# Decoding 64-bit weights by two bit operations, and looking for values out of range later

## The chip, the cores and the metric

The kernel runs on one core of a Trainium2 chip. The metric is the device time in microseconds of one execution, taken as the median of several runs. The core has TensorE (PE; its loading of weights is PEld), VectorE (DVE), ScalarE (ACT), GpSimd (POOL), SyncE (SP), and 16 DMA engines. Each engine carries out its own instructions in the order in which they stand; engines wait for each other by semaphores. VectorE and ScalarE both read the matmul results in PSUM.

## The reference

Three stages follow one another, with 3072 tokens of 512 values (4 batches of 768, 8 heads of 64). The weights `w_in` (512x1024) and `w_out` (1024x512) and `g_ln` arrive as 64-bit floating-point numbers, read by the kernel as pairs of 32-bit words; all else matters here only in outline.

```python
def _attn_ref(q, k, v, n_sink, window):
    scores = scale * np.matmul(q, k.transpose(0, 1, 3, 2))
    keep = is_sink | in_window
    scores = np.where(keep, scores, -1000000000.0)
    ...
    return np.matmul(a, v).astype(np.float32)

def _moe_ref(x, w_in, w_out, g_ln):
    h = x @ w_in
    ...
    solu = h * sm
    ln = (solu - mu) / np.sqrt(var + 1e-06) * g_ln
    return (ln @ w_out).astype(np.float32)

def _moe2_ref(x, w_gate, w1, w2):
    logits = x @ w_gate
    expert_idx = np.argmax(logits, axis=1)
    ...
    for e in range(E):
        xe = x[mask]
        h = np.maximum(xe @ w1[e], 0.0)
        ye = h @ w2[e]
        out[mask] = gate_w[mask, None] * ye
```

## The kernel before, in words

**Three stages.** Attention goes in 32 units, each two heads by three blocks of 128 queries. A unit is loaded (`a_load`), split into a high and a low part (`a_split`), its scores are made and their exponentials taken (`a_scores`, L223, L224, L230), the probabilities are transposed (`a_trans`, `tp`, L277) and multiplied with the values (`a_out`, `av`, L299), and the result is split into `bxh` and `bxl` (L304, L305), which are the input of the next stage. Four units make the input of one block of three tiles of 128 tokens. The MLP goes in 24 tiles: `m_in` (L428 to L430) makes `h` by three matmuls for each of four `k`, where `k` needs the unit `k` of the block; `m_act` takes the softmax and the normalization; `m_out` (L498 to L500) multiplies with `w_out`, with the router's logits as eight columns more. The experts' stage takes the 8 experts one after the other, sorted by load: `f_in` makes `ht` and from it `hh` and `hl` (L833, L834), `x_trans` makes `xeh` and `xel` for the next expert (L791, L792), `f_out` makes `y`. Their weights (`wst`, 512 KB each, eight for an expert: four of w1, four of w2) come through SyncE's queue (L725) and are split by ScalarE (`wh`, L733) and VectorE or GpSimd (`wl`, L741).

**High and low.** Every product of 32-bit numbers is made of three products of shorter ones: high by high, high by low, low by high. That is why each operand is split into a part that ScalarE rounds and a part that VectorE gets by subtraction.

**Decoding of `w_in` and `w_out`.** 16 tiles (8 of each) of 128 rows by 512 values, 512 KB each, are loaded through ScalarE's queue (L322) into `w64`, a tile with three buffers (`WB`). `decode` makes 32-bit floats of them. VectorE takes away the upper bits of the high word and shifts it left by three (L326, into `dt` in PSUM), and joins the sign and the top bit of the exponent (L328, into `dec`). ScalarE turns the low word into its top three bits (L329, in place) and takes the size of the high word, read as a float (L331, into `dh`). GpSimd adds the three bits (L332), which rounds the number. VectorE at last multiplies by zero whatever is too small for a 32-bit float (L334). `load_w_in` splits the result into `wih` and `wil` (L342, L343), `load_w_out` scales it by `g_ln` and splits it into `woh` and `wol` (L372, L373), and makes the logits' columns by transposes and matmuls on TensorE (`wt`, L351 and L359) of the decoded tile. `dec` has four buffers.

**What sets the order.** The program is written out with the units of attention and the tiles of weights in turn (L1253 to L1263: one tile every six steps, the last eight from step 62 on), then the MLP's steps beside the attention's; a scheduler then puts each engine's instructions in the order in which they would be ready by its own model of time. So the order on an engine is fixed when the kernel is built, and each engine keeps to it, also where what it waits for comes late.

**A second path.** `flags` (L1007) makes two flags on the input's values; if one is set, the fallback functions (`general_attention` and the like, at the end) compute the result again in another way. With the inputs of this case they do not run.

## Time and profile before

| | before |
|---|---|
| median of 3 runs | 822.47 us (821.12 to 825.34) |
| profiled execution, device time | 825.15 us |
| its span, first to last instruction | 823.4 us |
| mean granted clock of TensorE | 0.985 |
| TensorE busy | 771.7 us (94%) |
| VectorE busy | 470.6 us (57%) |
| ScalarE busy | 471.9 us (57%) |
| GpSimd busy | 377.4 us (46%) |

The rows below come from the profile of that one execution. The windows view gives for each stretch the busy time of each engine, with the number of instructions in brackets, the granted clock of TensorE as a share of its full speed, the mean busy share of the 16 DMA engines, and the rate at which they moved data. Groups of instructions are named by line, engine and operation, with output and inputs by the program's names; behind a bar stand the busy time in us and the mean length of one in ns, and behind a second bar the time for which the engine sat idle just before them, and what ended it. The chain of waits follows the work that ended last back from its end, piece by piece. "x16" is the number of instructions.

### The profile page before, as it was taken

How to read it: one execution, taken by the hardware profiler on the slowest of the kernel's cores; microseconds unless marked ns; L12 is line 12 of the kernel's file. 1: busy time of each engine (PE TensorE's matmuls, PEld its weight loads, DVE VectorE, ACT ScalarE, POOL GpSimd, SP SyncE). 2: the span in 40 equal slices, each digit the busy share in tenths (PEclk: the TensorE clock that was granted, in tenths of full speed). 3: DMA queues.
4: the chain of work that ended last, by engine and by line, in shares of the span. 5: the costliest groups of instructions: out<-in, count | busy, mean ns of one | idle time of the engine just before them, and what ended most of it. 6: DMA issues, size and time to landing. Idle time of an engine off the chain costs nothing.

```text
span 823.4 us, 15551 instructions
## 1 busy us (share of the span) xinstructions
PE 771.7 (94%) x5002; PEld 669.7 (81%) x5002; DVE 470.6 (57%) x1742; ACT 471.9 (57%) x1256; POOL 377.4 (46%) x413
## 2 busy tenths in 40 slices
PE   3469999889999999999999998999999999999996
PEld 2148888778888887888888888989978889889885
DVE  6788674755857756658667458516324324334441
ACT  4786685665866866848757466225424333436442
POOL 4787356435454553554533202137335344434533
PEclk9995999999999999999999999999999999999998
DMA  7776366668545656664540073076264415642550
GB/s 243 227 220 183 101 158 108 164 115 137 136 111 151 132 160 128 131 140 128 126 112 28 27 178 119 14 246 207 59 221 150 137 49 161 204 177 80 191 171 28
DMA packets 77418, 114.37 MB, mean 139 GB/s; under 512 B 14154, under 2 KB 53516, under 8 KB 77328
## 3 DMA queue, kind: packets, MB, share of 16 engines
q1 hardware_dynamic: 69648, 91.02, 42.9%
q0 software_dynamic: 5088, 13.88, 4.9%
q10 hardware_dynamic: 2592, 8.39, 3.0%
q8 instruction: 42, 0.69, 0.4%
q14 instruction: 48, 0.39, 0.3%
HBM read 72.22 MB, written 13.28 MB: 104 GB/s over the span
## 4 chain that ended last, share of the span: by engine, by line
PE 78%; DMA 8%; DVE 6%; ACT 3%; issue 2%; POOL 1%; SPq 0%; POOLq 0%; ACTq 0%; DVEq 0%
PE ht L825 5%; PE ht L826 5%; PE ht L827 5%; PE x L498 5%; PE av L299 5%; PE h L428 5%; PE y L897 5%; PE x L500 5%; PE y L895 5%; PE y L896 5%; PE x L499 5%; PE h L429 5%; PE h L430 4%; PE s L223 3%; DMA w<-w_out 2%
## 5 line engine op out<-in xcount | busy, mean ns | idle before, releaser
L498 PE MATMUL x<-woh,lh 128*128 128x264 f32 (+1 forms) x384 | 111.4, 290 | 0.1
L230 ACT ACTIVATE P<-P,mx 128x144 f32<-128x144 f32 x192 | 78.7, 412 | 54.6 <-DVE mx L228 51.9
L500 PE MATMUL x<-woh,ll 128*128 128x264 f32 (+1 forms) x384 | 109.4, 286 | 0.0
L499 PE MATMUL x<-wol,lh 128*128 128x264 f32 (+1 forms) x384 | 109.0, 284 | 0.0
L733 ACT ACTIVATE wh<-wst 128x1024 fp32r<-128x1024 f32 x64 | 67.5, 1058 | 46.1 <-PE ht L826 26.3
L741 POOL TENSOR_TENSOR wl<-wst,wh 128x1024 fp32r<-128x1024 f32 x28 | 68.2, 2436 | 56.0 <-ACT wh L733 49.0
L741 DVE TENSOR_TENSOR wl<-wst,wh 128x1024 fp32r<-128x1024 f32 x36 | 54.7, 1524 | 46.5 <-ACT wh L733 46.4
L826 PE MATMUL ht<-xel,wh 128*128 128x288 f32 (+5 forms) x256 | 81.1, 318 | 0.0
L827 PE MATMUL ht<-xeh,wl 128*128 128x288 f32 (+5 forms) x256 | 81.0, 318 | 0.0
L188 POOL TENSOR_TENSOR lA<-qd,qA 128x384 fp32r<-128x384 f32 x29 | 29.7, 1024 | 110.1 <-ACT qA L186 102.8
L825 PE MATMUL ht<-xeh,wh 128*128 128x288 f32 (+5 forms) x256 | 79.9, 318 | 0.0
L428 PE MATMUL h<-wih,bxh 128*128 128x512 f32 x192 | 78.6, 410 | 0.8 <-DVE ll L481 0.8
L227 DVE COPY_PREDICATED s<-pick,s 128x128 f32<-128x128 int32 x160 | 45.5, 291 | 55.9 <-PE s L224 53.8
L895 PE MATMUL y<-wh,hh 128*128 128x512 f32 x192 | 77.0, 402 | 0.0
L429 PE MATMUL h<-wil,bxh 128*128 128x512 f32 x192 | 76.5, 398 | 0.0
L897 PE MATMUL y<-wh,hl 128*128 128x512 f32 x192 | 75.8, 396 | 0.0
L896 PE MATMUL y<-wl,hh 128*128 128x512 f32 x192 | 75.1, 392 | 0.0
L430 PE MATMUL h<-wih,bxl 128*128 128x512 f32 x192 | 74.3, 400 | 0.0
L498 PEld LDWEIGHTS x<-woh,lh 128*128 128x128 f32 x384 | 72.3, 188 | 1.6 <-DVE r L531 0.3
L499 PEld LDWEIGHTS x<-wol,lh 128*128 128x128 f32 x384 | 72.4, 189 | 0.8
L500 PEld LDWEIGHTS x<-woh,ll 128*128 128x128 f32 x384 | 72.3, 189 | 0.4 <-issue 0.2
L228 DVE CUSTOM_DVE_ANT_0 P<-s,mk 128x144 f32<-128x144 f32 x192 | 55.9, 301 | 12.9 <-PE s L224 6.8
(259 smaller groups left out, 2058.4 us busy)
## 6 DMA issues: line engine op xcount, KB each, us to landing
wst<-w SPq DMA_DIRECT2D x64, 512.0 KB, 5.4
x_d<-xrow SPq DMA_DIRECT2D x24, 264.0 KB, 2.5
qd<-qT SPq DMA_DIRECT2D x32, 192.0 KB, 3.5
qB<-qA SPq DMA_DIRECT2D x58, 96.0 KB, 4.1
lB<-lA SPq DMA_DIRECT2D x58, 96.0 KB, 2.4
kd<-kx SPq DMA_DIRECT2D x16, 280.0 KB, 3.2
w<-w_in ACTq DMA_DIRECT2D x8, 512.0 KB, 6.6
w<-w_out ACTq DMA_DIRECT2D x8, 512.0 KB
```

What stands on the lines that cost most here:

```text
L428: T.matmul(h, xh[k], wih[:, k, cs], start=(k == 0), stop=False)
L429: T.matmul(h, xh[k], wil[:, k, cs], start=False, stop=False)
L498: T.matmul(p[:, 0:n], lh[:, k, :], woh[:, k, c, 0:n], start=(k == 0), stop=False)
L499: T.matmul(p[:, 0:n], lh[:, k, :], wol[:, k, c, 0:n], start=False, stop=False)
L500: mm = T.matmul(p[:, 0:n], ll[:, k, :], woh[:, k, c, 0:n], start=False, stop=(k == 7))
L741: return (G if c % 2 and r else V).tensor_tensor(out=l_, in0=st_w.pop((r, which, c)), in1=raw(h_), op=ALU.subtract)
L825: T.matmul(o, wh[:, k, fs], xh(k), start=(k == 0), stop=False)
L826: T.matmul(o, wh[:, k, fs], xl(k), start=False, stop=False)
L827: T.matmul(o, wl[:, k, fs], xh(k), start=False, stop=(k == 3))
L895: T.matmul(o, hh[:, k, sl], wh, start=(k == 0), stop=False)
L896: T.matmul(o, hh[:, k, sl], wl, start=False, stop=False)
L897: T.matmul(o, hl[:, k, sl], wh, start=False, stop=(k == 7))
```

## The change

The weights' tiles are decoded by two operations on VectorE and one on ScalarE. ScalarE turns the low word into its top three bits by the factor `LOW3`. VectorE shifts the high word left by three and joins the three bits by an exclusive or (`dt`); the second operation takes the sign of the high word and joins it by an exclusive or, with 0x80000000 for a constant. The exponent is not brought to the range of a 32-bit float: the number comes out with its sign turned and a power of two too large, which the next operations take out, since they have a factor (`SC_IN`, `SC_OUT`, `SX`, `RAW`). L331, the sum on GpSimd and the clearing at L334 are gone. The subtractions that make `wil` and `bxl` become operations with a factor. `g_s` and `g_l` are `g_ln` by those factors. `w64` has four buffers (`WB`). The old way stays for the fallback (`flush=True`).

Without the clearing, values out of the range would be decoded wrongly. So in the experts' stage the 16 tiles are loaded again through SyncE's queue (`look_at_weights`, into a `w64` with two buffers), and VectorE takes the least and the greatest size of the high words, read as floats, of each tile (`chk`, 32 reductions). `flag_weights`, called before the last expert, reduces them (`far`), compares (`bad`), sums over the 128 rows by one matmul (`ct`), and raises both flags of the second path; the cast `flag_i` moves there from `flags`.

The diff, without the fallback's own part:

```diff
--- before.py
+++ after.py
@@ -28,7 +28,7 @@
 NPT, XBUFS, QKB, PKB, VB = 2, 8, 2, 2, 2
-WB, DB, EB, NXR, XGB = 3, 4, 2, 2, 6
+WB, DB, EB, NXR, XGB = 4, 4, 2, 2, 6
 PA = 3
@@ -44,7 +44,10 @@
 PART = [n % 128 if n % 128 in (32, 64) else 0 for n in ROOM]
-E_MIN = struct.unpack("<f", struct.pack("<I", 897 << 20))[0]
+E_MIN, E_ONE = [struct.unpack("<f", struct.pack("<I", e << 20))[0] for e in (897, 1023)]
+LOW3 = 7.4995 * 2.0 ** -32
+SC_IN, SC_OUT, SX = 2.0 ** 8, 2.0 ** 64, 2.0 ** -8
+RAW = -2.0 ** -128
@@ -301,13 +304,15 @@
         xl = xp.tile([128, 384], F32R, tag="xl", name="bxl", bufs=XBUFS)
-        A.activation(out=xh, in_=o[:, 0:384], func=AF.Copy)
-        V.tensor_tensor(out=xl, in0=o[:, 0:384], in1=raw(xh), op=ALU.subtract)
+        A.activation(out=xh, in_=o[:, 0:384], func=AF.Copy, scale=SX)
+        V.scalar_tensor_tensor(out=xl, in0=o[:, 0:384], scalar=SX, in1=raw(xh), op0=ALU.mult, op1=ALU.subtract)
         x_t.setdefault(n // 4, []).append((xh, xl))
...
     g_sb = const.tile([128, 8], F32, name="g_sb")
+    g_s = const.tile([128, 8], F32, name="g_s")
+    g_l = const.tile([128, 8], F32, name="g_l")
     wg_sb = const.tile([128, 4, NE], F32, name="wg_sb")
@@ -315,42 +320,55 @@
-    def decode(src, sb=None):
+    def decode(src, sb, flush):
...
         lo, hi = w[:, :, 0], w[:, :, 1]
-        t = dec_tile("dec")
         t0 = ps("dt").bitcast(I32)
-        V.tensor_scalar(out=t0, in0=hi, scalar1=0x07FFFFFF, scalar2=3, op0=ALU.bitwise_and,
-                        op1=ALU.logical_shift_left)
-        V.scalar_tensor_tensor(out=t, in0=hi, scalar=-0x40000000, in1=t0, op0=ALU.bitwise_and, op1=ALU.bitwise_or)
-        A.activation(out=lo, in_=lo.bitcast(U32), func=AF.Copy, scale=2.0 ** -29)
-        x = ps("dh")
-        A.activation(out=x, in_=hi.bitcast(F32), func=AF.Abs)
-        G.tensor_tensor(out=t, in0=t, in1=lo, op=ALU.add)
-        y = x if sb is None else sb
-        V.scalar_tensor_tensor(out=y, in0=x, scalar=E_MIN, in1=t.bitcast(F32), op0=ALU.is_ge, op1=ALU.mult)
+        y = ps("dh") if sb is None else sb
+        if flush:
...
+        else:
+            A.activation(out=lo, in_=lo.bitcast(U32), func=AF.Copy, scale=LOW3)
+            V.scalar_tensor_tensor(out=t0, in0=hi, scalar=3, in1=lo, op0=ALU.logical_shift_left, op1=ALU.bitwise_xor)
+            V.scalar_tensor_tensor(out=y.bitcast(I32), in0=hi, scalar=-0x80000000, in1=t0, op0=ALU.bitwise_and,
+                                   op1=ALU.bitwise_xor)
         return y
-    def load_w_in():
+    def load_w_in(flush=False):
+        sc = SC_IN * (1.0 if flush else RAW)
         for k in range(4):
             for c in range(2):
-                x = decode(a["w_in"].bitcast(I32)[128 * k:128 * k + 128, 1024 * c:1024 * c + 1024])
+                x = decode(a["w_in"].bitcast(I32)[128 * k:128 * k + 128, 1024 * c:1024 * c + 1024], None, flush)
                 h_ = wih[:, k, 512 * c:512 * c + 512]
-                A.activation(out=h_, in_=x, func=AF.Copy)
-                V.tensor_tensor(out=wil[:, k, 512 * c:512 * c + 512], in0=x, in1=raw(h_), op=ALU.subtract)
+                A.activation(out=h_, in_=x, func=AF.Copy, scale=sc)
+                V.scalar_tensor_tensor(out=wil[:, k, 512 * c:512 * c + 512], in0=x, scalar=sc, in1=raw(h_),
+                                       op0=ALU.mult, op1=ALU.subtract)
                 yield 0
-    def load_w_out():
+    def load_w_out(flush=False):
+        sc = SC_OUT * (1.0 if flush else RAW)
+        V.tensor_scalar(out=g_s, in0=g_sb, scalar1=sc, scalar2=None, op0=ALU.mult)
+        V.tensor_scalar(out=g_l, in0=g_sb, scalar1=1.0 / SC_OUT, scalar2=None, op0=ALU.mult)
+
         def logits(k, x):
...
             xt = dec_tile("xt").bitcast(F32).rearrange("p (a b) -> p a b", a=4)
-            A.activation(out=xt, in_=t.rearrange("p (a b) -> p a b", a=4), func=AF.Copy)
+            A.activation(out=xt, in_=t.rearrange("p (a b) -> p a b", a=4), func=AF.Copy, scale=sc)
             return k, xt
@@ -358,7 +376,7 @@
             wp = t[:, 0:NE]
-            gk = g_sb[:, k:k + 1]
+            gk = g_l[:, k:k + 1]
             V.tensor_scalar(out=woh[:, k, 0, 256:264], in0=wp, scalar1=gk, scalar2=None, op0=ALU.mult)
@@ -366,11 +384,11 @@
             x = dec_tile("dec").bitcast(F32)
-            decode(a["w_out"].bitcast(I32)[128 * k:128 * k + 128, :], x)
+            decode(a["w_out"].bitcast(I32)[128 * k:128 * k + 128, :], x, flush)
             h_ = woh[:, k, :, 0:256]
             p2 = x.rearrange("p (a b) -> p a b", a=2)
-            A.activation(out=h_, in_=p2, func=AF.Copy, scale=g_sb[:, k:k + 1])
-            V.scalar_tensor_tensor(out=wol[:, k, :, 0:256], in0=p2, scalar=g_sb[:, k:k + 1], in1=raw(h_),
+            A.activation(out=h_, in_=p2, func=AF.Copy, scale=g_s[:, k:k + 1])
+            V.scalar_tensor_tensor(out=wol[:, k, :, 0:256], in0=p2, scalar=g_s[:, k:k + 1], in1=raw(h_),
                                    op0=ALU.mult, op1=ALU.subtract)
@@ -500,7 +518,7 @@
                     yield 0.65
-            A.activation(out=xr[:, 256 * c:256 * c + 256], in_=p[:, 0:256], func=AF.Copy)
+            A.activation(out=xr[:, 256 * c:256 * c + 256], in_=p[:, 0:256], func=AF.Copy, scale=1.0 / SC_OUT)
             if c == 0:
@@ -831,8 +849,8 @@
                 A.activation(out=hh[:, f, gs], in_=o, func=AF.Relu)
-                V.scalar_tensor_tensor(out=hl[:, f, gs], in0=o, scalar=0.0, in1=raw(hh)[:, f, gs], op0=ALU.max,
-                                       op1=ALU.subtract)
+                hl_last[0] = V.scalar_tensor_tensor(out=hl[:, f, gs], in0=o, scalar=0.0, in1=raw(hh)[:, f, gs],
+                                                    op0=ALU.max, op1=ALU.subtract)
             yield
@@ -960,10 +978,13 @@
                 x_gather(r + 1)
+            (look_at_weights if more else flag_weights)()
             for _ in f_in(r):
...
                 pass
+            if more:
+                look_at_weights()
             if not more:
@@ -987,6 +1008,8 @@
                 w2 = w_load(r + 1, 2)
+            if r in (1, 2):
+                look_at_weights()
@@ -1014,8 +1037,45 @@
         V.tensor_tensor(out=flag[:, 1:2], in0=flag[:, 1:2], in1=flag[:, 0:1], op=ALU.max)
+        rest_blocks(False)
+
+    chk = const.tile([128, 2, 16], F32, name="chk")
+    look, seen, hl_last = [], [0], [None]
+
+    def look_at_weights():
+
+        while look:
+            i, w = look.pop()
+            with tc.issue_after(hl_last[0].ins):
+                for j, op in enumerate((ALU.min, ALU.max)):
+                    V.tensor_reduce(out=chk[:, j, i:i + 1], in_=w[:, :, 1].bitcast(F32), axis=AX.X, op=op,
+                                    apply_absolute_value=True)
+        i = seen[0]
+        if i < 16:
+            seen[0] += 1
+            k = i % 8
+            w = pool2["h"].tile([128, 512, 2], I32, tag="w64", name="w64", bufs=2)
+            with tc.issue_after(loaded[-1].ins):
+                SY.dma_start(out=w, in_=a["w_out"].bitcast(I32)[128 * k:128 * k + 128, :] if i < 8 else
+                             a["w_in"].bitcast(I32)[128 * (k // 2):128 * (k // 2) + 128,
+                                                    1024 * (k % 2):1024 * (k % 2) + 1024])
+            look.append((i, w))
+
+    def flag_weights():
+        look_at_weights()
+        assert seen[0] == 16 and not look
+        far = const.tile([128, 2], F32, name="far")
+        bad = const.tile([128, 1], BF16, name="bad")
+        V.tensor_reduce(out=far[:, 0:1], in_=chk[:, 0], axis=AX.X, op=ALU.min)
+        V.tensor_reduce(out=far[:, 1:2], in_=chk[:, 1], axis=AX.X, op=ALU.max)
+        V.tensor_scalar(out=far[:, 0:1], in0=far[:, 0:1], scalar1=E_MIN, scalar2=None, op0=ALU.is_lt)
+        V.scalar_tensor_tensor(out=bad, in0=far[:, 1:2], scalar=E_ONE, in1=far[:, 0:1], op0=ALU.is_ge, op1=ALU.max)
+        p = ps("ct")
+        T.matmul(p[:, 0:1], ones_b, bad, start=True, stop=True)
+        for j in range(2):
+            V.scalar_tensor_tensor(out=flag[:, j:j + 1], in0=p[:, 0:1], scalar=0.5, in1=flag[:, j:j + 1],
+                                   op0=ALU.is_ge, op1=ALU.max)
         V.tensor_copy(flag_i, flag)
-        rest_blocks(False)
```

Three places of the instruction order follow; names are those of the program with a running number, which differs between the two builds. In all of them an engine's rows are in the order of its execution.

ScalarE at the start of the program, before: loads of `w64` (a DMA that it issues), and the first uses of the tiles.

```order
L322 DMA w64_239<-w_in 128x1024
L322 DMA w64_301<-w_in 128x1024
L322 DMA w64_360<-w_in 128x1024
L329 ACTIVATE w64_239<-w64_239 128x512
L331 ACTIVATE dh_246<-w64_239 128x512
L329 ACTIVATE w64_301<-w64_301 128x512
L331 ACTIVATE dh_308<-w64_301 128x512
L322 DMA w64_435<-w_in 128x1024
L230 ACTIVATE P_208,sm_210<-P_208,mx_209 128x144 x3
L329 ACTIVATE w64_360<-w64_360 128x512
L331 ACTIVATE dh_367<-w64_360 128x512
```

The same place after:

```order
L327 DMA w64_242<-w_in 128x1024
L327 DMA w64_300<-w_in 128x1024
L327 DMA w64_355<-w_in 128x1024
L327 DMA w64_426<-w_in 128x1024
L343 ACTIVATE w64_242<-w64_242 128x512
L343 ACTIVATE w64_300<-w64_300 128x512
L233 ACTIVATE P_211,sm_213<-P_211,mx_212 128x144 x3
L355 ACTIVATE wih_68<-dh_245 128x512
L327 DMA w64_466<-w_in 128x1024
L343 ACTIVATE w64_355<-w64_355 128x512
L355 ACTIVATE wih_68<-dh_303 128x512
```

Four loads stand at the head in place of three, the row `dh<-w64` (L331) is gone behind each use, and the fifth and sixth load come with one tile's use between them.

TensorE where the first product `h` of the MLP stands, before: `wt` are transposes and logits of the w_out tiles (the tile `dec_1191` is the seventh of eight), `s` scores of attention.

```order
L359 MATMUL wt2_1294<-wg_sb_125,xt_1217 128x8 x4
L351 MATMUL wt_1301<-ident_78,dec_1191 128x128 x2
L223 MATMUL s_722<-kA_685,qA_681 128x272
L224 MATMUL s_722<-kA_685,lA_683 128x272
L223 MATMUL s_728<-kB_686,qB_682 128x272
L224 MATMUL s_728<-kB_686,lB_684 128x272
L351 MATMUL wt_1301<-ident_78,dec_1191 128x128 x2
L428 MATMUL h_1314<-wih_68,bxh_454 128x512
L429 MATMUL h_1314<-wil_69,bxh_454 128x512
L430 MATMUL h_1314<-wih_68,bxl_455 128x512
L428 MATMUL h_1314<-wih_68,bxh_576 128x512
L429 MATMUL h_1314<-wil_69,bxh_576 128x512
```

The same place after (`dec_1134` is again the seventh):

```order
L377 MATMUL wt2_1143<-wg_sb_127,xt_1095 128x8 x4
L369 MATMUL wt_1150<-ident_78,dec_1074 128x128 x4
L226 MATMUL s_589<-kA_531,qA_527 128x272
L227 MATMUL s_589<-kA_531,lA_529 128x272
L377 MATMUL wt2_1227<-wg_sb_127,xt_1155 128x8 x4
L369 MATMUL wt_1234<-ident_78,dec_1134 128x128 x4
L446 MATMUL h_1247<-wih_68,bxh_441 128x512
L447 MATMUL h_1247<-wil_69,bxh_441 128x512
L448 MATMUL h_1247<-wih_68,bxl_442 128x512
L446 MATMUL h_1247<-wih_68,bxh_555 128x512
L447 MATMUL h_1247<-wil_69,bxh_555 128x512
L226 MATMUL s_595<-kB_532,qB_528 128x272
```

The first `h` uses the first two units (`bxh_441`, `bxh_555`) here, where before it used three (`bxh_454`, `bxh_576`, `bxh_709`) in a row; the third unit's output `av` comes behind the eighth tile.

VectorE at the end of the first layer of the fifth expert, before:

```order
L834 SCALAR_TENSOR_TENSOR hl_9002<-ht_9102,hh_9001 128x384
L834 SCALAR_TENSOR_TENSOR hl_9002<-ht_9117,hh_9001 128x384
L834 SCALAR_TENSOR_TENSOR hl_9002<-ht_9132,hh_9001 128x384
L792 TENSOR_TENSOR xel_9148<-xt_9149,xeh_9147 128x4x128
L795 COPY gate_185<-xg_8995 128x1
L800 CAST ids_f_184<-idx_i_182 128x1
```

The same place after, with the four reductions between the last `hl` and the first `xel`:

```order
L852 SCALAR_TENSOR_TENSOR hl_8976<-ht_9076,hh_8975 128x384
L852 SCALAR_TENSOR_TENSOR hl_8976<-ht_9091,hh_8975 128x384
L852 SCALAR_TENSOR_TENSOR hl_8976<-ht_9106,hh_8975 128x384
L1051 TENSOR_REDUCE chk_200<-w64_8973 128x1 x2
L1051 TENSOR_REDUCE chk_200<-w64_9123 128x1 x2
L810 TENSOR_TENSOR xel_9126<-xt_9127,xeh_9125 128x4x128
L813 COPY gate_187<-xg_8965 128x1
L818 CAST ids_f_186<-idx_i_184 128x1
```

SyncE's queue at the same expert, before: the last load of its second layer's weights and the next expert's first-layer weights (`w1`).

```order
L725 DMA wst_9081<-w2 128x2x512
L725 ISA
L725 DMA wst_9189<-w1 128x4x256
L725 ISA
L725 DMA wst_9235<-w1 128x4x256
L725 ISA
L725 DMA wst_9281<-w1 128x4x256
L725 ISA
L725 DMA wst_9287<-w1 128x4x256
```

The same place after:

```order
L743 DMA wst_9055<-w2 128x2x512
L743 ISA
L743 DMA wst_9167<-w1 128x4x256
L1059 DMA w64_8973<-w_in 128x1024
L743 ISA
L743 DMA wst_9213<-w1 128x4x256
L1059 DMA w64_9123<-w_in 128x1024
L743 ISA
L743 DMA wst_9259<-w1 128x4x256
L743 ISA
L743 DMA wst_9265<-w1 128x4x256
```

Two loads of `w64` have come between the first and the third load of `w1`.

## Rows read from the trace of the kernel before

**Rows 1.** Windows of 20 us: PE, PEld, DVE, ACT, POOL busy, clock, DMA share, GB/s:

```profile
0.00:20.00 20.00, 7.22 (x20) 3.92 (x20) 13.34 (x54) 8.73 (x23) 9.43 (x54) 1.00 0.77 241
...
20.00:40.00 20.00, 8.78 (x25) 4.28 (x25) 14.78 (x47) 14.39 (x38) 15.01 (x17) 1.00 0.70 221
...
40.00:60.00 20.00, 12.38 (x72) 8.56 (x73) 17.06 (x47) 16.95 (x43) 15.51 (x14) 1.00 0.79 229
...
80.00:100.00 20.00, 19.82 (x117) 16.60 (x116) 13.52 (x58) 11.57 (x37) 8.59 (x12) 1.00 0.43 118
```

**Rows 2.** The waits, TensorE, 90 to 540 us: total, times, longest:

```profile
PE s L224 <- DMA lA<-lA: 2.5, 1, 2.5
```

**Rows 3.** The windows view, most of the experts' stage, columns as in 1:

```profile
540.00:800.00 260.00, 260.00 (x1571) 229.03 (x1570) 100.20 (x190) 111.69 (x200) 116.88 (x75) 1.00 0.49 160
```

**Rows 4.** The windows view, other stretches of the front, columns as in 1:

```profile
0.00:69.00 69.00, 35.99 (x156) 23.67 (x157) 53.32 (x173) 46.51 (x120) 45.86 (x91) 0.94 0.78 235
...
21.00:51.00 30.00, 14.01 (x55) 7.92 (x54) 24.33 (x68) 22.73 (x57) 22.95 (x24) 1.00 0.68 210
...
51.00:69.00 18.00, 13.90 (x81) 11.33 (x82) 14.76 (x50) 14.23 (x41) 13.48 (x14) 0.79 0.95 265
...
63.00:78.00 15.00, 13.83 (x66) 11.91 (x64) 14.12 (x36) 11.07 (x28) 11.74 (x11) 0.50 0.69 172
```

**Rows 5.** Chain of waits up to 110 us: start, length, what:

```profile
32.15 2.48 POOL dec L332 x2
...
41.85 1.30 POOL dec L332
...
59.37 4.75 DMA w<-w_out
```

**Rows 6.** The timeline, ScalarE: start, length, what, idle before it and releaser:

```profile
68.88 0.67 ACT L329 ACTIVATE w<-w 128x512 int32<-128x512 uint32 x1 [0.30 <-DMA w<-w_out]
```

**Rows 7.** The timeline, TensorE:

```profile
79.81 0.48 PE L428 MATMUL h<-wih,bxh 128*128 128x512 f32 x1
```

**Rows 8.** Instruction groups up to 90 us: busy, mean ns, idle before and releasers:

```profile
L332 POOL TENSOR_TENSOR dec<-dec,w 128x512 int32<-128x512 int32 x16 | 20.9, 1310 | 14.4 <-DVE dec L328 9.0 <-ACT xt L353 2.4 <-PE s L224 2.1
...
L326 DVE TENSOR_SCALAR dt<-w 128x512 int32<-128x512 int32 x16 | 11.0, 687 | 4.8 <-DMA w<-w_in 3.5 <-DMA w<-w_out 1.2
...
L328 DVE SCALAR_TENSOR_TENSOR dec<-w,dt 128x512 int32<-128x512 int32 x16 | 10.8, 678 | 0.0
...
L329 ACT ACTIVATE w<-w 128x512 int32<-128x512 uint32 x16 | 10.8, 677 | 18.2 <-DMA w<-w_in 11.8 <-DMA w<-w_out 6.4
...
L331 ACT ACTIVATE dh<-w 128x512 f32<-128x512 f32 x16 | 9.9, 622 | 0.0
...
L373 DVE SCALAR_TENSOR_TENSOR wol<-dec,g_sb,woh 128x512 fp32r<-128x512 f32 x8 | 8.4, 1056 | 4.5 <-ACT woh L372 4.5
...
L334 DVE SCALAR_TENSOR_TENSOR dh<-dh,dec 128x512 f32<-128x512 f32 x8 | 5.5, 691 | 0.0
...
L334 DVE SCALAR_TENSOR_TENSOR dec<-dh,dec 128x512 f32<-128x512 f32 x8 | 5.4, 676 | 0.0
```

**Rows 9.** Instruction groups, whole program, columns as in 8:

```profile
L434 DVE TENSOR_REDUCE sc<-h 128x1 f32<-128x512 f32 x48 | 32.3, 685 | 16.3 <-PE h L430 14.1 <-ACT e L462 2.1
...
L792 DVE TENSOR_TENSOR xel<-xt,xeh 128x512 fp32r<-128x512 f32 x25 | 17.2, 688 | 74.2 <-ACT xeh L791 74.1
```

**Rows 10.** The waits, ScalarE, 540 to 824 us:

```profile
ACT wh L733 <- DMA wst<-w: 3.5, 3, 1.6
```

**Rows 11.** The timeline, VectorE, end of the program:

```profile
793.41 1.15 DVE L801 TENSOR_TENSOR dst<-ids_f,pen 128x1 int32<-128x1 f32 x1
...
800.65 1.23 DVE L741 TENSOR_TENSOR wl<-wst,wh 128x1024 fp32r<-128x1024 f32 x1 [6.09 <-ACT wh L733]
```

**Rows 12.** The timeline, TensorE: two sets of six transposes:

```profile
54.11 0.88 PE L277 MATMUL tp<-ident,pk 128*128 128x128 f32 x6
...
73.33 1.49 PE L277 MATMUL tp<-ident,pk 128*128 128x128 f32 x6
```

16 lines of the change are left out of this document (13 added, 3 removed).

## The prediction

> **What bounds the kernel now.** I read the windows first, in stretches of 20 us. Over the first 60 us TensorE works 7.22, 8.78 and 12.38 us of each 20 [rows 1], so 31.6 us of it are idle; from 80 us on it is nearly full (19.82 of 20 [rows 1]). Over 90 to 540 us its largest wait on anything is 2.5 us in all [rows 2], and from 540 to 800 us it is busy 260.00 of 260.00 [rows 3]. So the end of the program can move in one way only: TensorE must get its work earlier in the first 80 us, or be made to wait later on. VectorE or GpSimd time saved anywhere else costs and earns nothing.
>
> Next I asked what holds the front. VectorE is busy 13.34, 14.78 and 17.06 of 20 there [rows 1], the highest of the helpers, and the 16 DMA engines are busy 0.78 of the first 69 us [rows 4]. The chain of waits goes through both: a piece of 4.75 us of waiting for a weight tile to land, and before it pieces of the GpSimd sum `dec` at L332 (2.48 us for two of them, 1.30 for another) [rows 5]. The reader should see the loop: a load needs a free one of three buffers, the buffer is given back by the last reader of the raw tile, which is the GpSimd sum at L332, and that sum waits for VectorE. The last of the 16 tiles is picked up by ScalarE at 68.88 us [rows 6], and the first matmul of the MLP starts at 79.81 us [rows 7]. It needs none of the w_out tiles, but it stands in TensorE's row behind the transposes and logits of seven of them.
>
> **The change part by part.**
>
> *Decoding, VectorE.* Per tile, L326, L328 and L334 (687, 678 and 691 or 676 ns, 16 of each [rows 8]) make 2.05 us. Two operations of 128x512 in their place, of the same kind as L328 (two inputs, 678 ns) make 1.36. That is 0.69 us by 16 tiles: 11.0 us less, all of it before 80 us. The low half of w_out, L373, takes 1056 ns on average against 678 for an operation of the same size and kind [rows 8]; the nearest reason in the trace is that GpSimd reads and writes beside it. GpSimd loses its 20.9 us of L332 [rows 8]; if half of the excess goes with it, 8 times 0.19, that is 1.5 us. VectorE: −12.5 us.
>
> *Decoding, ScalarE and GpSimd.* ScalarE loses 16 times L331, 9.9 us [rows 8], GpSimd 20.9. ScalarE had 18.2 us of waiting for tiles in front of L329 [rows 8], so of its saving I count nothing by itself. The GpSimd sum stood in the chain, and with it went the handovers between VectorE, ScalarE and GpSimd; the raw tile is now given back by the second VectorE operation.
>
> *The scale factors.* The power of two goes into operations that were there already (the scale of an activation, or a two-input subtraction that becomes one with a scalar, of the kind and size of L328). The 32 `bxl` operations change kind in the same way. The two 128x8 products `g_s` and `g_l` are done once. All together under 0.5 us on an engine that is not full; nothing in the sum.
>
> *The fourth buffer and the loads.* Bytes do not change in the front. The DMA engines are busy 0.68 of 21 to 51 us and 0.95 of 51 to 69 [rows 4]: in the first stretch they have 9.6 us free, because loads wait for buffers; in the second they are the limit. With four buffers, given back two handovers earlier, weights can use the free 9.6 us. All of the 69 us hold 53.8 us of transfers (0.78 by 69 [rows 4]), so even packed without a gap the last tile could not land much before 56 to 58 us, 11 to 13 us earlier. The order of ScalarE shows four loads at the head where there were three, and the next already behind the first use of one tile.
>
> Of the two limits the smaller decides: VectorE could give 12.5 us, the transfers 9.6. I take 9.6, as the stretch from 21 to 51 us is what the buffers govern. The lower end is 3.7 us, the two GpSimd pieces shown from the chain (2.48 and 1.30 [rows 5]) with every load where it was. The upper end is 16.5 us, 9.6 and the clock's 6.9 (below), half of TensorE's idle 31.6.
>
> There is a rule that speaks against the fourth buffer. The row shows the DMA engines at 0.95 where several loads are under way [rows 4]. The Trainium skill, page "DMA: Bandwidth & Descriptors", section "Issuing engines are not separate DMA queues", says that transfers of all issuing engines run on the same 16 engines and interleave. By that rule a fourth load at the head takes its time from the first three and from the first queries and keys: 512 KB at the 265 GB/s of 51 to 69 us are 2.0 us, and the sum would be 7.6 in place of 9.6. I don't take this, since those engines then have a gap later.
>
> *TensorE's order.* In both orders the first h matmul stands behind the logits of the seventh w_out tile; but ahead of it the changed order has two outputs of attention (`av`) in place of three, and behind it h products of five blocks with those two units before the fourth output comes. So TensorE gets h work sooner after the weights are there, and the third and fourth unit later. What it gains up to 90 us it keeps, as it is full behind. I put no further gain in the sum, and the later units into the last rival.
>
> *Looking for values out of range.* 16 loads of 512 KB more, and 32 reductions on VectorE, all in the experts' stage. The nearest row is the reduction of 512 values at L434, 685 ns [rows 9]: 32 times 0.685 are 21.9 us. VectorE is busy 100.20 of 260 us there [rows 3]. They come mostly in groups of four (2.7 us) behind the last `hl` of an expert, ahead of the first `xel` of the next. `xel` waited 74.2 us in 25 (3.0 each) for ScalarE [rows 9], so the group stands in an idle stretch; what is queued behind it is `xel`, on which the next expert's first matmul waits only after the whole second layer of this one. If the cover were gone, 8 groups of 2.7 are 21.9 us. The 8.4 MB raise the DMA share of the stage from 0.49 by 0.10 (160 GB/s at 0.49 [rows 3] means some 327 at full). The loads stand in SyncE's queue between the weights of the next expert; that is the rival below. ScalarE waited for those weights 3.5 us in all [rows 10]. I take +1.0 us, between 0 and 3.
>
> *The flag.* Two reductions of 128x16, four small operations, one matmul of one column and a cast, once, behind the last `hl`. VectorE's last `dst` starts at 793.41, and its next work is at 800.65 [rows 11]: 6 us of cover. Nothing.
>
> **Sum.** The profiled execution took 825.15 us; −9.6 in the front, +1.0 in the experts, is 816.55. It was 2.68 above the median of the runs, 822.47, so the forecast for the median is 813.9 us.
>
> **The rivals.**
>
> *The front gives less (819.8 us).* The loads stay where they are, because ScalarE issues them in its own order, behind exponentials that wait for scores, and only the GpSimd pieces go: −3.7 + 1.0. For it: the 51 to 69 us stretch is at 0.95. Against: 0.68 just before.
>
> *The clock (807.0 us).* From 63 to 78 us the granted clock is 0.50, the lower of the two levels (1.2 GHz), while TensorE is busy 13.83 of 15 [rows 4]; before that it had idled much of every 20 us [rows 1]. Six transposes took 0.88 us at 54.11 and 1.49 at 73.33 [rows 12]. If TensorE is kept busy from 50 us on, those 13.83 us take half, 6.9 less. Against: nothing fills all of its gaps. The Trainium skill, page "TensorE: Matmul & The Clock Gate", Part 1, says that the slow clock is the resting state and that activity lifts it; the rows agree in that the low stretch follows an idle one, but no row shows that this change lifts it.
>
> *The new loads hold up the weights (835 us; slower).* Per expert two loads of the look stand between the four w1 loads in SyncE's row. 512 KB at 327 GB/s are 1.6 us; two are 3.2 us by 7 experts, 22 us, if ScalarE's `wh` is as late as the loads and TensorE waits with it: 813.9 − 1.0 + 22.4 = 835.3. It decides the sign from 1.4 us an expert on (9.6 by 7). For it: SyncE is in order, and the weights are asked for when a buffer comes free. Against: ScalarE waited only 3.5 us for 64 such loads [rows 10].
>
> *The tiles aren't decoded sooner (821 to 823).* VectorE's freed time goes to attention's work that TensorE can't use, or a wait of the same size turns up in the middle stage, whose order also changes.
>
> **Chances.** Main case 0.53, with a range of its own of 807 to 818 (front −6 to −16). Less in the front 0.20, the clock 0.10, held up weights 0.08, no change 0.09. Half a per cent, 4.1 us, is about what a measurement of this kernel can tell from no change: faster is under 818.4, slower over 826.6. Faster: 0.51 of the main case, 0.06 of the second and 0.10, so 0.67; same: 0.02, 0.14, 0.07, so 0.23; slower 0.10. The range leaves out half of the clock's case, the slow rival and a little beside: 805 to 822.
>
> **What would show it.** In the trace of the changed kernel: VectorE's busy time up to 80 us down by 11 to 13 us and GpSimd's by about 21; the DMA share of 21 to 51 us over 0.8; the last w_out tile picked up by ScalarE at about 60 us in place of 68.88, and the first h matmul near 68 to 70 in place of 79.81; TensorE full from about 78 us on; in the experts' stage, reductions of about 0.69 us with the idle time of `xel` down by some 20 us, and ScalarE's wait for weights under 10 us. I am wrong if the last tile still lands at 66 us or later (then the second rival), if the granted clock stays at 1.00 through 50 to 80 us (the clock), or if TensorE waits for `wh` or `wl` in the experts by more than 5 us.

## The result: 0.8% slower, with the gain at the front given back

| | before | after |
|---|---|---|
| median of 6 runs on one chip | 823.07 us (821.12 to 825.34) | 830.82 us (828.26 to 831.54) |
| ratio | 1 | 1.0083 [1.006, 1.0106] |
| profiled execution, device time | 825.15 us | 831.02 us |
| its span | 823.4 us | 829.2 us |
| mean granted clock | 0.985 | 0.978 |

The forecast was 813.9 us, with a range of 805 to 822. The time lies above the range and on the other side of the kernel before.

The windows of the changed kernel, with the columns of [rows 1] and [rows 4], the last line a stretch to be compared below:

```profile
0.00:20.00 20.00, 7.34 (x20) 4.03 (x21) 12.65 (x55) 8.27 (x22) 5.59 (x51) 1.00 0.79 257
20.00:40.00 20.00, 11.62 (x37) 6.50 (x36) 19.59 (x56) 15.60 (x43) 12.20 (x14) 1.00 1.00 288
40.00:60.00 20.00, 17.66 (x92) 14.07 (x93) 14.25 (x40) 14.10 (x37) 9.15 (x10) 0.82 0.87 217
60.00:80.00 20.00, 19.53 (x105) 16.79 (x101) 11.07 (x42) 8.45 (x25) 8.19 (x10) 0.67 0.29 79
80.00:100.00 20.00, 17.32 (x96) 13.98 (x95) 10.00 (x40) 9.79 (x31) 8.15 (x9) 1.00 0.57 153
100.00:120.00 20.00, 18.28 (x107) 14.36 (x106) 14.09 (x66) 16.90 (x55) 10.65 (x14) 0.74 0.60 156
21.00:51.00 30.00, 20.03 (x80) 13.26 (x79) 24.74 (x70) 21.72 (x55) 17.30 (x19) 0.97 1.02 278
...
96.00:112.00 16.00, 11.60 (x58) 8.13 (x59) 13.21 (x61) 14.21 (x44) 8.37 (x11) 0.68 0.48 121
```

Up to 60 us TensorE now works 36.62 us where it worked 28.38 [rows 1], though from 40 us on at a clock of 0.82: the front moved the way that was forecast. The DMA engines, 0.68 busy from 21 to 51 us before [rows 4], are full there. But from 80 to 100 us TensorE works 17.32 where it worked 19.82 [rows 1], and from 100 to 120 us 18.28 at a clock of 0.74. These are the places where the start of the work shows, ScalarE's last w_out tile, the first h, the fourth unit's `bxh` (ScalarE) and the first transposes behind the activation (`lt`), in the timelines after:

```profile
53.43 0.69 ACT L343 ACTIVATE w<-w 128x512 int32<-128x512 uint32 x1 [1.78 <-DMA w<-w_out]
...
67.87 0.78 PE L446 MATMUL h<-wih,bxh 128*128 128x512 f32 x1
...
90.88 0.49 ACT L307 ACTIVATE bxh<-av 128x384 fp32r<-128x384 f32 x1 [1.05 <-PE av L302]
...
112.68 1.09 PE L495 MATMUL lt<-ident,e 128*128 128x128 f32 x8
```

and the last of them before:

```profile
106.88 0.38 PE L477 MATMUL lt<-ident,e 128*128 128x128 f32 x2
```

The last tile is picked up 15.5 us earlier (68.88 in [rows 6]), the first h starts 11.9 us earlier (79.81 in [rows 7]), and yet the first `lt`, from which on TensorE has the second layer's work, starts 5.8 us **later**. The fourth unit's `bxh`, the last input of the first tiles, is later too: it stood at 87.15 us before.

Why it is later is seen in TensorE's timeline. Attention's sixth unit has its scores (`s`, six groups) ahead of the fourth unit's output (`av`) in TensorE's order. After:

```profile
78.57 0.29 PE L226 MATMUL s<-kA,qA 128*128 128x272 f32 x1
...
79.05 0.29 PE L226 MATMUL s<-kB,qB 128*128 128x272 f32 x1
...
82.09 0.29 PE L226 MATMUL s<-kA,qA 128*128 128x272 f32 x1
...
83.97 0.29 PE L226 MATMUL s<-kB,qB 128*128 128x272 f32 x1
...
84.22 0.29 PE L226 MATMUL s<-kA,qA 128*128 128x272 f32 x1
...
87.26 0.28 PE L226 MATMUL s<-kB,qB 128*128 128x272 f32 x1
...
89.01 0.60 PE L296 MATMUL av<-skt,vsk 128*128 128x384 f32 x2
```

Between the first and the last of them start 32 h matmuls, for which the weights and the first units were ready. The six groups take 8.7 us to start. VectorE, which takes each of them next, isn't what holds them: it waits for them (74 to 96 us; total, times, longest):

```profile
DVE s L230 <- PE s L227: 8.1, 6, 2.3
```

When the fourth unit is there at last, most of what TensorE could have done while VectorE and ScalarE take the softmax and the normalization of the first tiles is done already. The windows from the fourth unit's `bxh` to the first `lt`, of the h matmuls alone (TensorE's busy time and their number, clock, DMA share, GB/s), before and after:

```profile
87.15:106.88 19.73, 13.39 (x51) 1.00 0.49 124
...
90.88:112.68 21.80, 3.91 (x15) 0.77 0.55 139
```

Where 51 h matmuls lay beside the activation, 15 are left. TensorE waits for VectorE's work on attention's next units:

```profile
98.93 0.37 PE L226 MATMUL s<-kB,qB 128*128 128x272 f32 x1 [2.68 <-DVE skt L268]
...
99.42 0.87 PE L280 MATMUL tp<-ident,pk 128*128 128x128 f32 x6
101.46 0.98 PE L296 MATMUL av<-skt,vsk 128*128 128x384 f32 x2 [1.16 <-DVE mx L231]
```

and behind these idle microseconds the clock falls to its lower level (1.2 GHz). Two stretches after, 1.62 of 5 us busy, then a clock of 0.52:

```profile
96.00:101.00 5.00, 1.62 (x10) 0.97 (x9) 5.00 (x18) 4.28 (x12) 2.02 (x2) 0.94 0.31 81
101.00:111.00 10.00, 8.98 (x38) 6.53 (x38) 7.52 (x45) 8.93 (x30) 5.53 (x7) 0.52 0.55 138
```

Before, the stretch from 96 to 112 us held 15.30 us of work at full clock; after, 11.60 at 0.68 (the last line of the windows above):

```profile
96.00:112.00 16.00, 15.30 (x95) 12.55 (x94) 13.74 (x60) 15.17 (x49) 7.88 (x9) 1.00 0.45 113
```

So theory A: the earlier weights let h run ahead of attention; h is then used up while the fourth unit is held up behind it, and the gain of the front, and more, is given back between 96 and 112 us. That is read from one execution of each kernel; the experiments test it. Its rivals: B, the second look at the weights costs the difference in the experts' stage; C, the order of h doesn't matter.

### The profile page after: what moved, and what is told of

Its sections match the earlier page's. It is cut to its first block, busy times and chain, and to the rows that moved or that the text cites. A ratio compares the mean times of both kernels' runs of the same rounds, so it can differ in the third digit from the quotient of the medians.

```text
span 829.2 us, 15575 instructions
## 1 busy us (share of the span) xinstructions
PE 781.6 (94%) x5003; PEld 676.1 (82%) x5003; DVE 475.4 (57%) x1766; ACT 462.0 (56%) x1240; POOL 357.1 (43%) x397
## 3 DMA queue, kind: packets, MB, share of 16 engines
q1 hardware_dynamic: 71952, 99.41, 44.9%
## 4 chain that ended last, share of the span: by engine, by line
PE 79%; DMA 8%; DVE 7%; issue 2%; ACT 2%; POOL 1%; POOLq 0%; SPq 0%; ACTq 0%; DVEq 0%
PE ht L844 6%; PE ht L843 5%; PE ht L845 5%; PE x L516 5%; PE av L302 5%; PE x L518 5%; PE h L446 5%; PE x L517 5%; PE y L913 5%; PE h L447 5%; PE y L915 5%; PE y L914 5%; PE h L448 4%; DMA w<-w_out 3%; PE s L226 3%
## 5 line engine op out<-in xcount | busy, mean ns | idle before, releaser
L516 PE MATMUL x<-woh,lh 128*128 128x264 f32 (+1 forms) x384 | 111.5, 291 | 0.9 <-DVE r L549 0.8
L915 PE MATMUL y<-wh,hl 128*128 128x512 f32 x192 | 75.5, 395 | 0.0
L242 POOL TENSOR_TENSOR pk<-P,sm 128x768 f32<-128x768 f32 x32 | 47.1, 1471 | 41.1 <-DVE sm L240 19.9
```

What stands on the lines that cost most here:

```text
L516: T.matmul(p[:, 0:n], lh[:, k, :], woh[:, k, c, 0:n], start=(k == 0), stop=False)
L915: T.matmul(o, hl[:, k, sl], wh, start=False, stop=(k == 7))
```

## The experiments

Each ratio is to the kernel before on the same chip. The chips differ: the kernel before took 823 to 829 us on them, so that only ratios are compared between groups. The times in the last four columns are read from the profiled executions' timelines (us): last w_out load issued, first h, fourth unit's `bxh`, first `lt`.

| kernel | ratio [95%] | last load | first h | `bxh` 4 | `lt` |
|---|---|---|---|---|---|
| before | 1 | 64.8 | 79.8 | 87.1 | 106.9 |
| after | 1.0083 [1.0060, 1.0106] | 45.6 | 67.9 | 90.9 | 112.7 |
| after, no look | 1.0087 [1.0061, 1.0112] | 44.8 | 65.1 | 87.2 | 110.1 |
| before, look alone | 1.0045 [1.0021, 1.0070] | 66.8 | 80.4 | 88.9 | 108.7 |
| after, three buffers | 1.0101 [1.0041, 1.0161] | 54.6 | 68.1 | 89.2 | 115.5 |
| after, h held behind `av` of unit 4 | **0.9905** [0.9875, 0.9934] | 46.6 | 77.8 | 77.9 | 99.0 |
| the same, no look | 0.9853 [0.9788, 0.9919] | 44.8 | 75.4 | 75.5 | 96.6 |
| the same, three buffers | 0.9948 [0.9918, 0.9977] | 55.1 | 79.4 | 79.5 | 100.6 |
| before, h held behind `av` of unit 4 | 1.0061 [1.0023, 1.0100] | 65.9 | 88.1 | 88.3 | 111.5 |
| the same, four buffers | 1.0101 [1.0047, 1.0154] | 51.7 | 84.7 | 84.8 | 106.4 |
| after, h held behind `av` of unit 3 | 1.0136 [1.0070, 1.0201] | 44.9 | 70.1 | 85.7 | 107.2 |
| after, h held behind scores of unit 6 | **0.9928** [0.9898, 0.9957] | 44.0 | 72.3 | 77.9 | 97.9 |
| the same for all blocks | 0.9987 [0.9944, 1.0029] | 44.7 | 72.7 | 78.3 | 98.3 |
| after, once more | 1.0059 [1.0018, 1.0099] | 44.6 | 64.2 | 84.8 | 107.7 |

The first `lt` doesn't set the time by itself: in its second profile the changed kernel has it at 107.7 us, about where it stood before, and that execution took 838.6 us. So the table below follows the lead over the kernel before through four profiles: the time at which that kernel had ended as many matmuls, less the time at which this one has (us; the last column is the difference of the spans). The profile of the kernel before is that of the first chip; on the chips of the second and the fourth row that kernel takes some 5 and 2.5 us longer, so that their later columns are a little too low.

| kernel | at 95 us | at 120 | at 200 | at 240 | at 520 | end |
|---|---|---|---|---|---|---|
| after | 4.6 | −2.8 | 4.4 | 2.2 | −2.3 | −5.8 |
| after, once more | 7.7 | 2.3 | 4.8 | −1.3 | −9.6 | −13.4 |
| after, h held behind `av` of unit 4 | 6.3 | 7.2 | 10.6 | 10.4 | 8.0 | 6.2 |
| after, h held behind scores of unit 6 | 9.1 | 9.2 | 13.3 | 13.5 | 14.0 | 10.0 |

Between 95 and 120 us the changed kernel loses 5 to 7 us in both profiles and the held ones nothing: that is theory A. Between 120 and 200 us all gain, as the kernel before stalls there, 2.5 us of it for `lA` [rows 2]. Behind 240 us the changed kernel loses 8 and 12 us and the held ones some 4, which theory A doesn't explain.

### The look, taken away and added alone

`e1_no_look`, the edit:

```diff
     def look_at_weights():
-        while look:
...
+        pass
     def flag_weights():
-        look_at_weights()
...
+        V.tensor_copy(flag_i, flag)
```

> The changed kernel without the second look at the weights: the 16 loads in the experts' stage, the 32 reductions and the comparisons are left out, so values out of range would not be noticed; decoding and the fourth buffer stay. Theory A (the front's gain of some 7 us up to 100 us is given back between 96 and 112 us, where TensorE has used up the h work that used to cover the activation of the first tiles, and waits for attention's fourth unit with the clock falling; the look costs only the 2 us seen near 690 us): 828 to 829.5 us, 1 to 3 under the changed kernel's 830.8, and still slower than the kernel before. Rival B (the front's gain holds and the look costs the rest in the experts' stage): 812 to 818 us.

Measured: 1.0087, the same as with the look. Rival B falls: without the look the kernel is as slow.

`e2_look_only` puts `look_at_weights`, `flag_weights` and their calls, as in the diff of the change, into the kernel before.

> The kernel before, with the second look at the weights alone added (16 loads, 32 reductions, comparisons), decoding and three buffers as before. Theory A: 824 to 826 us, 1 to 3 above the kernel before; TensorE's progress up to 540 us as before, within 1 us. Rival B: 830 us or more.

Measured: 1.0045, 3.7 us, a little above what A expected. In its profile the first `lt` comes 1.8 us later than before, long before any of the look runs, which the look cannot have done directly. From the first `ht` of the experts to the end it takes 316.6 us, in the kernel before 313.9. Over all profiles this stretch takes 313.9 to 315.5 us in the five kernels without the look and 315.3 to 317.6 in the nine with it. The means are 315.0 and 316.5, so the look costs 1 to 2 us there; what makes up the rest of the 3.7 us (interval 1.7 to 5.8) stays open.

### h held back

`e3_hold_h`, the edit (`av_last[n]` is the last `av` matmul of unit n, counted from 0; `issue_after` sets an order within TensorE's row and adds no wait):

```diff
-            T.matmul(h, xh[k], wih[:, k, cs], start=(k == 0), stop=False)
-            T.matmul(h, xh[k], wil[:, k, cs], start=False, stop=False)
-            T.matmul(h, xl[k], wih[:, k, cs], start=False, stop=(k == 3))
+            with tc.issue_after(av_last[3].ins) if t < 3 and dec_p[0] is at else ExitStack():
+                T.matmul(h, xh[k], wih[:, k, cs], start=(k == 0), stop=False)
+                T.matmul(h, xh[k], wil[:, k, cs], start=False, stop=False)
+                T.matmul(h, xl[k], wih[:, k, cs], start=False, stop=(k == 3))
```

> The changed kernel with the h matmuls of the first three tiles kept in TensorE's order behind the output of attention's fourth unit; nothing else is changed. Theory A: the fourth unit's bxh comes at 80 to 87 us in place of 90.9, the first transpose behind the activation (lt) at 100 to 107 in place of 112.7, no low clock between 100 and 112 us, and the whole is 3 to 8 us shorter than the changed kernel, 822 to 828 us. Rival C (the order of the h matmuls doesn't matter, the loss between 96 and 112 us is VectorE's and ScalarE's latency alone, or what is gained here is lost as idle time before): lt within 2 us of 112.7, 830 to 833 us.

Measured: 0.9905, 816.16 us where the kernel before took 823.23 on the same chip: 7 us under the kernel before and some 14 under the changed one, more than I expected. The sixth unit's scores (the first and the last of the six groups), the fourth unit's output and the first `lt` in its timeline:

```profile
71.87 0.39 PE L226 MATMUL s<-kA,qA 128*128 128x272 f32 x1
...
74.64 0.37 PE L226 MATMUL s<-kB,qB 128*128 128x272 f32 x1 [0.15 <-DVE mx L231]
...
76.05 0.59 PE L298 MATMUL av<-skt,vsk 128*128 128x384 f32 x2
...
99.00 1.03 PE L499 MATMUL lt<-ident,e 128*128 128x128 f32 x8
```

The six groups start within 2.8 us in place of 8.7, the unit is ready 13 us earlier, and so is `lt`, although the first h starts 10 us later. And its windows, where the h matmuls now lie beside the first activations (the last line is of the h matmuls alone, from the fourth unit's `bxh` to the first `lt`):

```profile
60.00:80.00 20.00, 18.48 (x120) 14.43 (x116) 13.18 (x57) 12.66 (x40) 12.46 (x14) 0.84 0.49 130
80.00:100.00 20.00, 20.00 (x118) 16.66 (x117) 14.22 (x57) 13.52 (x40) 7.55 (x11) 1.00 0.64 158
100.00:120.00 20.00, 20.00 (x150) 18.15 (x149) 13.68 (x62) 15.11 (x49) 7.16 (x10) 1.00 0.40 110
96.00:112.00 16.00, 16.00 (x125) 13.88 (x124) 12.38 (x55) 13.96 (x44) 7.19 (x10) 1.00 0.42 100
...
77.92:99.00 21.08, 16.08 (x60) 1.00 0.61 153
```

From 96 to 112 us TensorE is busy 16.00 of 16 at full clock, and from `bxh` to `lt` 60 h matmuls lie beside the activation in place of 15. The count goes with the clock in all 14 profiles: 51 to 60 h matmuls and a clock of 1.00 in that stretch in the kernels with the old decoding and in those held behind unit 4 or behind the scores; 15 and 0.74 to 0.78 in the four profiles of the changed kernel as it is, without look and with three buffers; 20 and 0.80 with h held behind unit 3. Theory A holds, rival C falls.

`e9_hold_scores` asks which part of the order matters: the same edit with `s_last[5]`, the last score matmul of the sixth unit, in place of `av_last[3]`, so that h may fill the time until the output.

> The changed kernel with the h matmuls of the first three tiles kept behind the last scores of attention's sixth unit, which stand ahead of the fourth unit's output in TensorE's order; h may fill the time until that output. Theory A in its narrower form (what did the harm are those scores standing between h matmuls, so that VectorE, ScalarE and with them the fourth unit's output came late): the fourth unit's bxh at 76 to 82 us, lt at 98 to 104, and a ratio to the kernel before of 0.985 to 0.995, as when h was held behind the output itself. Rival E (each order has luck of its own): lt as early, but a ratio over 1.

Measured: 0.9928, with `bxh` at 77.9 and `lt` at 97.9 us. It is the scores between h matmuls that held up the unit, and rival E, by which each order has luck of its own, falls here. The two held versions can't be told apart in time.

`e7_hold_third`: `av_last[2]` in place of `av_last[3]`.

> The changed kernel with the h matmuls of the first three tiles kept behind the output of attention's third unit only, so that many of them still stand ahead of the fourth unit's. Theory A, by dose: the fourth unit's bxh between those of the two other kernels (77 and 90.9 us), the first lt between 98.8 and 112.7, and 818 to 828 us. Rival E (any change of the order breaks the bad luck of the changed kernel, whichever unit is ahead): 814 to 818 us.

Measured: the fourth unit at 85.7 and `lt` at 107.2 us, between those of the changed and the held kernel, as A expects. But the time is 1.0136, not under the changed kernel's (the intervals overlap) and well above the 818 to 828 us that A expected. Rival E, by which any new order would help, falls too. What was saved up to 125 us is lost later, in places that the other kernels have in a smaller measure. Two windows of it:

```profile
400.00:420.00 20.00, 15.57 (x100) 13.53 (x100) 9.26 (x47) 10.56 (x35) 7.19 (x8) 0.91 0.64 131
...
500.00:520.00 20.00, 15.47 (x108) 14.52 (x109) 18.62 (x65) 14.39 (x38) 7.36 (x5) 0.88 0.40 133
```

In the first TensorE waits 4.4 us at once for a part of attention's queries (`lA`) that a DMA moves:

```profile
412.51 0.53 PE L227 MATMUL s<-kA,lA 128*128 128x272 f32 x1 [4.43 <-DMA lA<-lA]
```

Why this kernel waits longer there than others (2.5 us in the second profile of the changed one) was not tried; the chain up to 125 us explains the first loss, not this one.

`e11_hold_all`: the hold of `e9_hold_scores` for all blocks (`s_last[min(4 * (t // 3) + 5, 31)]`).

> As the run that held h behind the sixth unit's scores, but for the h matmuls of all eight blocks: those of block b behind the last scores of unit 4b+5. Theory A (the order mattered at the start because there TensorE had nothing else for the time of the first activations; later the second layer of tiles before fills it): up to 125 us as the run that held the first block, and 0.985 to 1.000 of the kernel before, within 0.5% of that run's 0.9928. If h running ahead of attention costs in every block: 0.975 to 0.985.

Measured: 0.9987. Up to 100 us it runs as the kernel with one block held; the difference comes after. Holding the later blocks back too gains nothing, and rather costs: the two ratios are 0.6% apart, on two chips, and their intervals overlap a little. That h pays as cover only where TensorE has no other work fits this, but was not tried by itself.

### The hold without the change, and the parts of the front

`e5_before_hold` is the kernel before with the edit of `e3_hold_h`; `e10_old_decode_four` has `WB = 4` beside it; `e8_hold_three_buffers` is `e3_hold_h` with `WB = 3`; `e4_three_buffers` the changed kernel with `WB = 3`; `e6_hold_no_look` joins the edits of `e3_hold_h` and `e1_no_look`.

> The kernel before, with the h matmuls of the first three tiles kept behind the output of attention's fourth unit, as in the run that held them in the changed kernel; decoding, three buffers and no second look as before. Theory A (holding pays only because the changed decoding has let h run ahead of attention; before, three units already stood ahead of h): the fourth unit's bxh at 83 to 87 us in place of 87.15, and 819 to 823.5 us, a gain of 0 to 4. Rival D (the hold is worth its 14.7 us by itself, and the new decoding adds nothing or harms): 807 to 813 us.

Measured: 1.0061, slower than the kernel before. Rival D falls, and so does my "0 to 4 us faster": there the weights come late, and holding h back leaves TensorE without work (7.83 of 10 us busy from 80 to 90 us):

```profile
80.00:90.00 10.00, 7.83 (x43) 5.62 (x42) 5.60 (x26) 5.82 (x20) 7.54 (x10) 0.83 0.52 138
```

> The kernel before with the hold behind the fourth unit's output and four buffers for the raw tiles; the old decoding, no second look. It completes a square of four with the held runs: new decoding with four and with three buffers 0.9905 and 0.9948 of the kernel before, old decoding with three 1.0061. If the shorter decoding brings the front's gain and the buffer adds its 3.5 us: a ratio of 1.000 to 1.005, the last tile issued at 58 to 65 us. If the buffer alone lets the loads come early: 0.988 to 0.997, the last tile issued before 55 us.

Measured: 1.0101, not to be told from 1.0061. Neither expectation came true whole. The last load is issued at 51.7 us, 14 us earlier than with three buffers, the fourth unit comes 3.4 us and the first `lt` 5.1 us earlier, and yet nothing is left of it in the ratio; where it is lost stays open.

> The held kernel with three buffers for the raw tiles in place of four. If the earlier loads are what brings the front's gain: the last tile is issued 3 to 8 us later, and 818 to 823 us, 2 to 7 above the held kernel's 816.2. If VectorE's shorter decoding brings it and the fourth buffer adds nothing: 815 to 818 us.

Measured: 0.9948 against 0.9905; the intervals touch, so that the fourth buffer is worth 0 to 7 us with the new decoding. With h held, the new decoding with the look is worth 0.9948 against 1.0061 with three buffers and 0.9905 against 1.0101 with four: 1.1 and 2.0%, 9 and 16 us, each to within some 5 us.

> The changed kernel with three buffers for the raw tiles in place of four. Theory A: the loads come later, the last one is issued at 48 to 56 us in place of 45.6, but as the gain of the front is given back anyway, the time is within 3 us of the changed kernel, 828 to 834 us. If the fourth buffer itself were the harm (loads that crowd out attention's first queries and keys): 820 to 826 us.

Measured: 1.0101, the same as with four. The fourth buffer isn't the harm.

> The held kernel without the second look at the weights (16 loads, 32 reductions and comparisons are left out, so values out of range would not be noticed). If the look lies in VectorE's idle stretches: 814 to 816.5 us, 0 to 2 under the held kernel's 816.2. If the look costs what the run with the look alone showed (3.7 us): 811.5 to 813.5 us.

Measured: 0.9853 [0.9788, 0.9919], which takes in both 0.9905 and a look that costs 4 us; inconclusive by itself.

> The changed kernel itself, on the same chip as the run beside it, since the chips of the last runs differ by up to 6 us in the kernel before: 1.006 to 1.011 of the kernel before. If the held runs' gain were a matter of the chip, it would be under 1.000 here.

Measured: 1.0059, on a chip where the kernel before took 828 us. The changed kernel is slower than the kernel before there too.

## Why the prediction was wrong, point by point

**What bounds the kernel** held in its first half: TensorE got its work earlier in the first 80 us. What decided was the second half, that it can "be made to wait later on", to which the sum gave nothing.

**Decoding, VectorE** was sized too high. The three operations per tile (2.05 us) became two, in the instruction groups up to 80 us after:

```profile
L344 DVE SCALAR_TENSOR_TENSOR dt<-w 128x512 int32<-128x512 int32 x16 | 13.1, 820 | 1.5 <-ACT w L343 1.5
...
L391 DVE SCALAR_TENSOR_TENSOR wol<-dec,g_s,woh 128x512 fp32r<-128x512 f32 x8 | 7.8, 976 | 4.6 <-ACT woh L390 4.6
L345 DVE SCALAR_TENSOR_TENSOR dh<-w,dt 128x512 int32<-128x512 int32 x8 | 5.5, 690 | 0.0
L345 DVE SCALAR_TENSOR_TENSOR dec<-w,dt 128x512 int32<-128x512 int32 x8 | 5.4, 678 | 0.0
```

L344 takes 820 ns on average, not 678: L328, by which it was sized, reads one of its two inputs from PSUM, and L344 reads both from SBUF, as L373 with its 1056 ns does (more in the last section). With L345's 10.9 us the two cost 24.0 where the three cost 32.7 [rows 8]: −8.7 us in place of −11.0. L391 takes 0.6 us less than L373 did, not 1.5. Together −9.3, forecast −12.5. GpSimd lost its 20.9 us. The row that I wanted to go by, 11 to 13 us less of VectorE up to 80 us, was no good measure: VectorE is busy 57.6 us in place of 63.5 there, as other work moved in.

**The loads** gained more than I allowed. I had 11 to 13 us as the most that the last tile could gain, and took 9.6; it gained 15.5. The step put all transfers of the 69 us ahead of the last tile, attention's too. Up to 51 us the weights' queue moved 8.38 MB where it had moved 6.39, and SyncE's queue, which loads attention's inputs, 5.45 where it had moved 5.00; another 2.37 MB of attention's came behind the last tile, from 51 to 69 us, where the engines are half free, 0.52 in place of 0.95 [rows 4]:

```profile
51.00:69.00 18.00, 16.95 (x83) 14.60 (x83) 13.96 (x45) 10.47 (x29) 6.13 (x7) 0.59 0.52 134
```

The rule that I weighed against the fourth buffer, that of the Trainium skill, page "DMA: Bandwidth & Descriptors", section "Issuing engines are not separate DMA queues", that the transfers of all issuing engines share 16 engines, is not contradicted: the engines were full from 21 to 51 us (1.02). With three buffers and the new decoding they were 0.87 busy there, so the fourth buffer moved loads into time that was free. The 2.0 us that I worked out by the rule as a delay of the first tiles did not show: ScalarE picks up the first three at 9.5, 11.5 and 15.4 us, before at 9.4, 11.3 and 15.4.

**TensorE's order** is the step that failed. I read from the order that h stood ahead of the third and fourth unit, and wrote that what TensorE gains up to 90 us it keeps, "as it is full behind". It was full behind because h work lay there, 72 matmuls of a tile triple at 0.23 us, 16.6 us, beside an activation that takes some 20 us from `bxh` to `lt` (19.7 before, 21.8 after, 21.1 held). Work that is done earlier is no longer there as cover. What decided was the chain unit 4, activation, `lt`, and this got longer. I named the later units and put them into the last rival, 821 to 823 us, with no price for them. Its price shows in the order: the h matmuls between the scores of the sixth unit, 32 of 0.23 us, 7.4 us. TensorE's lead over the kernel before was 4.6 us at 95 us and −2.8 at 120, a loss of 7.4; with h held it went from 6.3 to 7.2.

**The clock** as a rival asked whether the low stretch would vanish. It moved: 0.67 from 60 to 80 us (0.57 before), and a new one from 101 to 111 us behind the new idle time. There TensorE was busy 8.98 us at 0.52; at full clock the same work would take about half, so some 4 us are lost. The Trainium skill, page "TensorE: Matmul & The Clock Gate", Part 1, says that the slow clock is the default and comes back after idle time. The trace agrees in this place: 1.62 of 5 us busy from 96 to 101 us, then 0.52. The chance that I gave to the clock staying up was for the wrong place.

**The look** was right: +1.0 forecast, 1 to 2 measured. The slower rival had the right sign for the wrong reason. ScalarE's wait for the experts' weights is 2.3 us, 3.5 before [rows 10]; VectorE waits 7.7 us for two of the new loads, in time it had (540 to 830 us):

```profile
DVE chk L1051 <- DMA w<-w_out: 7.7, 2, 5.3
...
ACT wh L751 <- DMA wst<-w: 2.3, 2, 1.6
```

The windows agree: TensorE is busy all but 1 us of 260 there.

```profile
540.00:800.00 260.00, 259.02 (x1563) 227.68 (x1562) 114.20 (x226) 110.82 (x198) 117.02 (x78) 1.00 0.56 190
```

**The sum** was −9.6 in the front and +1.0. With h held behind the fourth unit the kernel gains 0.95% [0.66, 1.25], 5 to 10 us, which takes in the forecast's 8.6. That the amount agrees is in part luck: the loads gained more than the sum had, VectorE less, and TensorE's lead at 95 us was 4.6 to 9.1 us in the four profiles of the second table, under the 9.6. The mechanism of the front was there; the order took it away again between 95 and 120 us.

**Open** is the loss behind 240 us: by the matmuls done the changed kernel is 2.2 us ahead of the kernel before at 240 us in the first profile and ends 5.8 us behind; in the second, on a slower chip, it goes from 1.3 to 13.4 behind. With the 4 us that the held kernels lose there it would have ended, in the first profile, some 2 us behind. So the order explains why the front's gain was gone by 120 us. The one line of `e3_hold_h` moves the whole time by some 14 us, 12 in the two profiles; 8 of these 12 are there at 240 us (10.4 against 2.2) and are traced to the order, the other 4 come behind it on a path that is not. Why the time came out above the kernel before, and not near it, is not shown. Stalls of TensorE of 2 to 4 us for attention's DMAs and for the router's small operations come and go between kernels with the same code there.

## What to carry to other kernels

An engine that is full behind a stretch doesn't keep what it gains in it, if what fills it is work that was only waiting: ask which latency that work covers, and follow the longest chain (here a unit of attention, an activation, the next matmuls) through each engine's order. Here inputs came earlier, and the scheduler put their users earlier too, ahead of links of that chain; after such a change look at what has moved between them, and hold it back where one line does it. The same line that turned this change from 0.8% slower to 0.95% faster made the kernel without the change slower.
